# Attention backward and weight gradients: from two blocks under a scheduler to one hand-set order of slots

## The chip, the cores and the metric

One core of a Trainium2 chip runs the whole program. The metric is device time in microseconds (us) of one execution. Five engines take part, each with a queue of its own: TensorE (PE in the profile, its weight loads PEld), VectorE (DVE), ScalarE (ACT), GpSimd (POOL) and SyncE (SP), which issues most of the transfers.

## The reference

The forward pass of one block (layer norm, attention, residual, layer norm, MLP, residual) and the gradients of all its inputs. S = 2048 rows, D = 512, 32 heads of 16, F = 1792. Attention looks at 8 earlier positions, every second one:

```
idx  = pos[:, None] - off[None, :]          # off = 0, 2, ..., 14
kg, vg = k[:, :, idx], v[:, :, idx]
logits = einsum("bhsd,bhswd->bhsw", q, kg) * scale      # masked where idx < 0
o      = einsum("bhsw,bhswd->bhsd", softmax(logits), vg)
h      = x + o @ wo ;  h2 = h + gelu(ln(h) @ w1 + b1) @ w2 + b2
_out, _vjp = jax.vjp(_f, A_x, A_wqkv, A_wo, B_w1, B_b1, B_w2, B_b2)
```

The outputs are h2 and the gradients of x, wqkv, wo, w1, b1, w2 and b2.

## The kernel before

The rows are worked on in NC = 4 chunks of CH = 512. The program has a forward attention part, an MLP part (forward and backward, ending in `gh`, the gradient at h), and then the part that is changed: `p3_...`, the attention backward, and behind it the weight gradients. A scheduler sets the order of instructions on each engine from the order in which the code is written and from when buffers come free; engines wait on semaphores that it places.

Attention backward, for a chunk c:

- `p3_go(c)`: TensorE transposes `gh`, multiplies it with `woT` into `got` (features on partitions), and a row-major copy goes to `go_d` in HBM.
- `p3_gl(c, got)`: VectorE multiplies `got` with eight shifted views of `vw` (`dots`, tile `pr`, four of 4096 elements), TensorE sums over a head's features into `ps_ga`; `pp`, a row sum on TensorE, and `glf`, the gradient of the logits.
- `band`: the sums over the eight positions. A band is 256 rows; there are 2 each for the gradients of q, v and k of a chunk, 24 in all. SP loads `R`, 1.3 MB of shifted rows, in 4 transfers, into one of 3 buffers. VectorE multiplies `R` with coefficients `cf` (four of 2048 elements, tile `prb`, in two halves m), TensorE sums them with `S32`, ScalarE evicts into `gqs` or `gks`, which POOL's queue stores to `g3_d`. `coefs` makes `cf` by transposing pieces of `attn`, `glf` or `sh` on VectorE; `sh` is a copy shifted by position, four transfers (`p3_shift`).
- `p3_gq(c)`: the q bands. `p3_kv(c, shs)`: the v and k bands, `unperm` (transposes on TensorE) into `gqkvT`, then for each 128 rows 12 matmuls with `wqkvT` into `ps_gl1`, and `ln_bwd`: ScalarE makes `gyr`, POOL a small constant, VectorE four passes that end in `gx`, which SP stores.

The weight gradients each are sums over all 16 row tiles. gw2 (14 groups of 16 matmuls, lhs a tile `gtm` of 1 MB that a transposing transfer makes from `g_d`), gb2, gw1 (28 groups of 16 matmuls with 256 columns, tiles `ghm`), gwo (4 groups) and gwq (12 groups, from `g3_d`). `load_tm` loads the other operand, 2 MB, into the one buffer `r16`: `gout_r`, `ln2_r`, `o_r` and, in 32 transfers, `ln1_r`. `wg_out` evicts a group into one of two `gwst` buffers, and SP stores it. Transposed tiles have two buffers.

In the order as built, all of the weight gradients stand behind the last `ps_gl1` on TensorE. SP's queue holds, in one order, the loads of `R`, the shifts, the stores of `go_d`, `gx` and `gwst`, and the transposing loads; each of them waits there for what it needs.

## Time and profile before

| | |
|---|---|
| median of 3 runs | 985.37 us (985.09 to 988.18) |
| the profiled execution | 986.06 us, its span 984.1 us |
| mean granted TensorE clock | 0.835 |
| busy in the span | PE 695.0, DVE 535.2, ACT 336.1, POOL 87.3 us |
| moved by DMA | 146.09 MB, 148 GB/s on average |

The span runs from the first to the last instruction; durations of the trace belong to that one execution. The granted clock is a share of TensorE's full speed, and the DMA share is the mean busy share of the core's 16 DMA engines. A row of instructions has its start, its duration, engine, line, operation, result and operands, a count where several are merged, and in brackets the idle time before it and what ended that.

### The profile page before, as it was taken

To read this page: it belongs to the slowest core of one execution; us is meant where nothing else is said; L and a number is where in the kernel's file an instruction comes from. 1 tells how busy PE (TensorE), PEld (TensorE's weight loads), DVE (VectorE), ACT (ScalarE), POOL (GpSimd) and SP (SyncE) were. 2 spreads that over 40 slices of the span, in tenths; PEclk is the share of its full clock that TensorE was granted. 3 is DMA by queue.
4 is the path that set the end of the run, shared out by engine and by line. 5 is a ranking of instruction groups with operands and counts; after the bars stand their busy time and mean duration, and the time that the engine had idled before them with its cause. 6 is when DMAs were issued, how large, how long until landed. Compare 5 with 4: busy or idle time off the path is not lost.

```text
span 984.1 us, 10416 instructions
## 1 busy us (share of the span) xinstructions
PE 695.0 (71%) x3891; PEld 312.4 (32%) x3948; DVE 535.2 (54%) x814; ACT 336.1 (34%) x497; POOL 87.3 (9%) x137
## 2 busy tenths in 40 slices
PE   5777775547899898898556546537459775776788
PEld 2423332212334333333222212212114333664233
DVE  6778676458777787857767767777683000000000
ACT  2755664365346353414333233213222101111011
POOL 3211221200010010101000100100101000000000
PEclk9998897677999999999675785755659997997779
DMA  9646556851233242238848747747799986563211
GB/s 311 202 127 161 132 167 176 183 129 60 81 97 97 77 126 87 86 124 189 195 100 203 186 110 196 181 105 186 182 263 243 251 203 177 124 144 105 74 60 38
DMA packets 159599, 146.09 MB, mean 148 GB/s; under 512 B 96042, under 2 KB 150140, under 8 KB 155068
## 3 DMA queue, kind: packets, MB, share of 16 engines
q1 hardware_dynamic: 153196, 124.42, 49.2%
q0 software_dynamic: 6352, 20.99, 6.7%
q8 instruction: 31, 0.51, 0.2%
q14 instruction: 20, 0.16, 0.1%
HBM read 72.95 MB, written 47.80 MB: 123 GB/s over the span
## 4 chain that ended last, share of the span: by engine, by line
PE 29%; DMA 16%; DVE 10%; issue 5%; ACT 4%; SPq 4%; POOL 1%; DVEq 0%; ACTq 0%; POOLq 0%
DMA R<-q_d 5%; PE ps_gw L722 5%; PE ps_gw L707 4%; PE ps_gwq L755 4%; PE ps_gl L671 4%; DMA R<-go_d 3%; PE ps_f L533 2%; DVE prb L267 2%; DMA gtm<-g_d 2%; SPq L746 2%; PE ps_gg L546 2%; PE ps_gwo L729 2%; DMA R<-k_d 2%; DVE pr L236 2%; PE ps_go L612 1%
## 5 line engine op out<-in xcount | busy, mean ns | idle before, releaser
L267 DVE TENSOR_TENSOR prb<-R,cf 128x2048 bf16<-128x2048 bf16 x128 | 148.3, 1218 | 51.5 <-DMA R<-go_d 23.3
L272 PE MATMUL ps_band<-prb,S 128*32 128x512 bf16 x512 | 73.6, 564 | 116.3 <-DVE prb L267 113.2
L498 PE MATMUL ps_h<-ln2T,w 128*128 128x512 bf16 x223 | 63.4, 410 | 25.9 <-ACT x L501 22.4
L722 PE MATMUL ps_gw<-ghm,ln_r 128*128 128x256 bf16 x448 | 53.5, 284 | 22.3 <-ACT gwst L692 12.2
L272 PEld LDWEIGHTS <-S 128*32 128x32 bf16 x512 | 15.9, 100 | 162.1 <-DVE prb L267 105.5
L546 PE MATMUL ps_gg<-goT,w2T 128*128 128x512 bf16 x218 | 53.8, 378 | 11.4 <-DVE gb1p L549 8.6
L707 PE MATMUL ps_gw<-gout_r,gtm 128*128 128x512 bf16 x220 | 51.9, 396 | 12.9 <-DMA gtm<-g_d 12.7
L692 ACT ACTIVATE gwst<-ps_gw 128x256 bf16<-128x256 f32 (+1 forms) x42 | 18.5, 454 | 121.5 <-PE ps_gw L722 40.3
L755 PE MATMUL ps_gwq<-gtm,ln_r 128*128 128x512 bf16 x188 | 50.3, 427 | 9.9 <-DMA ln_r<-ln_d 9.7
L722 PEld LDWEIGHTS <-ln_r 128*128 128x128 bf16 x448 | 45.5, 102 | 30.5 <-issue 13.1
L533 PE MATMUL ps_f<-w,gt 128*128 128x512 bf16 x217 | 53.5, 383 | 1.1 <-DVE gt L510 0.5
L500 ACT ACTIVATE xb<-ps_h,b1c 128x512 bf16<-128x512 f32 x56 | 38.2, 685 | 45.5 <-PE ps_h L498 44.1
L330 PE MATMUL ps_qkv<-ln1T,wqkv 128*128 128x512 bf16 x184 | 47.5, 393 | 6.9 <-ACT kt L332 3.2
L671 PE MATMUL ps_gl<-wqkvT,gqkvT 128*128 128x512 bf16 x184 | 48.0, 414 | 0.2
L661 ACT ACTIVATE gks<-ps_band 128x512 bf16<-128x512 f32 x32 | 19.2, 600 | 82.7 <-PE ps_band L272 80.3
L208 ACT ACTIVATE gyr<-ps_gl,rstd 128x512 bf16<-128x512 f32 x32 | 21.9, 686 | 59.8 <-PE ps_gl L559 24.0
L498 PEld LDWEIGHTS <-w 128*128 128x128 bf16 x224 | 23.0, 103 | 60.0 <-issue 42.2
L501 ACT ACTIVATE x<-ps_h,b1c 128x512 bf16<-128x512 f32 x56 | 37.9, 684 | 9.0 <-DMA ln_d<-ln 6.9
L214 POOL TENSOR_SCALAR c<-sg 128x1 f32<-128x1 f32 x32 | 24.6, 769 | 172.7 <-ACT gyr L208 172.7
L236 DVE TENSOR_TENSOR pr<-qt,kt 128x4096 bf16<-128x4096 bf16 x16 | 36.0, 2284 | 5.7 <-ACT qt L332 3.5
L236 DVE TENSOR_TENSOR pr<-got,vw 128x4096 bf16<-128x4096 bf16 x16 | 35.6, 2287 | 1.3 <-DMA vw<-vf_d 1.3
L707 PEld LDWEIGHTS <-gtm 128*128 128x128 bf16 x224 | 22.4, 101 | 41.9 <-DMA gtm<-g_d 13.8
(312 smaller groups left out, 1080.2 us busy)
## 6 DMA issues: line engine op xcount, KB each, us to landing
R<-v_d SPq DMA_DIRECT2D x32, 320.0 KB, 5.0
R<-k_d SPq DMA_DIRECT2D x32, 320.0 KB, 5.1
R<-go_d SPq DMA_DIRECT2D x32, 320.0 KB, 7.5
R<-q_d SPq DMA_DIRECT2D x32, 320.0 KB, 10.8
g_d<-gt SPq DMA_DIRECT2D x12, 512.0 KB, 3.2
ln_d<-ln POOLq DMA_DIRECT2D x8, 512.0 KB, 6.0
out_dram<-gwst SPq DMA_DIRECT2D x30, 128.0 KB, 1.7
w<-in_B_w_dram POOLq DMA_DIRECT2D x2, 1792.0 KB, 11.2
```

Source lines behind the costliest of these rows:

```text
L236: V.tensor_tensor(out=pr[:], in0=ql[:, g, :].unsqueeze(1).to_broadcast([P, W, 512]), in1=_sub(kw_[:, g, PAD:PAD + 512], [[-DIL, W], [1, 51 ...
L267: V.tensor_tensor(out=pr[:, hf].rearrange("p j (d h) -> p j d h", h=H), in0=R[:, o:o + 4, :].rearrange("p j (d h) -> p j d h", h=H), in1=c ...
L272: T.matmul(ps[32 * j:32 * j + 32, :], lhsT=S32[:], rhs=pr[:, hf, j, :], start=(hf == 0), stop=(hf == 1), skip_group_check=True)
L330: T.matmul(ps[:, gg, :], lhsT=wqkv[:, dc, sel * D + g * P:sel * D + (g + 1) * P], rhs=st_[c]["ln1T"][:, dc, :], start=(dc == 0), stop=(dc ...
L498: T.matmul(ps[:, i, :], lhsT=w1[:, dc, f * P:(f + 1) * P], rhs=ln2T[c][:, dc, :], start=(dc == 0), stop=(dc == DC - 1))
L500: A.activation(out=xb[:, f - f0, :], in_=ps[:, i, :], func=ACT.Identity, bias=b1c[:, f:f + 1])
L533: T.matmul(ps[:], lhsT=gts[f // 4][:, f % 4, j * P:(j + 1) * P], rhs=w2[:, f, :], start=(f == 0), stop=False)
L546: T.matmul(ps[:, i, :], lhsT=w2T[:, dc, f * P:(f + 1) * P], rhs=goT[:, dc, :], start=(dc == 0), stop=(dc == DC - 1))
L671: T.matmul(ps[:], lhsT=gqkvT[:, b, j * P:(j + 1) * P], rhs=wqkvT[:, b, :], start=(b == 0), stop=(b == 11))
L707: T.matmul(ps[:], lhsT=gtm[:, t, (f % 2) * P:(f % 2 + 1) * P], rhs=r16[:, t, :], start=(t == 0), stop=(t == NT - 1))
L722: T.matmul(ps[:, 0:256], lhsT=r16[:, t, dc * P:(dc + 1) * P], rhs=ghm[:, t, :], start=(t == 0), stop=(t == NT - 1))
L755: T.matmul(ps[:], lhsT=r16[:, t, dc * P:(dc + 1) * P], rhs=g_[:, t, :], start=(t == 0), stop=(t == NT - 1))
```

## The change

The forward coefficients and those of the backward pass are transposed by fewer, larger instructions: `coefs` makes all of a chunk at once, in one instruction of 1024 elements from `sh`, in two of 512 from `glf` or `attn`.

Everything from the attention backward on stands in a manual schedule, so the order on each engine is that of the code. The code is written in slots. A slot has some VectorE work (one `dots` tile or one half band), then `slot(dve_us)`: it first runs the TensorE work that `later` put off to this slot (a band's sums, `unperm`, `p3_go` in pieces, `ps_gl1`), each with a cost, and then `filler`, which takes matmuls from the generator `wgrads` until `dve_us * 1.22` less those costs is used up. `wgrads` runs through gw2, gb2, gw1, gwo and gwq; a number that it yields is charged, 24.0, 14.0 or 6.0 after it has issued loads, and a name ("q", "v", "k") holds it until that gradient is stored. At the end `filler(1000.0)` issues the rest.

`ln_bwd` of chunk c-2 is spread over the dots of chunk c (`gln1`); chunks 2 and 3 have none over them. v bands come first, then q, then k; `R` is loaded two bands ahead (`load_R`). The stores of `gx`, of `gwst` and of gb1 are issued by POOL. gwq takes its second operand in halves of 1 MB in the buffers of the transposed tiles, where before all three were loaded into buffers of their own while gw2 ran.

```diff
+    def coefs(wp, src, off, hs):
+        cf = wp.tile([P, 2, 2, 8, H], BF16, name="cf", tag="cf", bufs=2)
+        if hs == 512:
+            V.transpose(out=cf[:].rearrange("p a b c h -> p (a b c h)"), in_=_sub(src, [[256, 4], [1, 8], [8, 32]], off))
+        else:
+            for hf in range(2):
+                V.transpose(out=cf[:, hf].rearrange("p b c h -> p (b c h)"),
+                            in_=_sub(src, [[256, 2], [1, 8], [8, 32]], off + hf * hs))
         return cf
...
+    ms = tc.manual_schedule()
+    ms.__enter__()
...
+    def wg_out(ps, dst, width=D, sca=1.0):
+        st = gwp.tile([P, D], BF16, name="gwst", tag="gwst", bufs=2)
+        A.activation(out=st[:, 0:width], in_=ps[:, 0:width], func=ACT.Copy, scale=sca)
+        G.dma_start(out=dst, in_=st[:, 0:width])
...
+    def load_t(src):
+        t_ = gwp.tile([P, NT, 256], BF16, name="gwm", tag="gwm", bufs=2)
+        SY.dma_start_transpose(out=t_[:], in_=src)
+        return t_
...
+    MM = 0.22
+
+    def wgrads():
+        r16 = load_tm("gout_r", gof)
+        tiles = [load_t(g_d[f * 256:(f + 1) * 256, :]) for f in range(2)]
+        yield 24.0
+        for f in range(FT):
+            gtm = tiles[f // 2]
+            ps = FY("ps_gw2")
+            for t in range(NT):
+                T.matmul(ps[:], lhsT=gtm[:, t, (f % 2) * P:(f % 2 + 1) * P], rhs=r16[:, t, :], start=(t == 0), stop=(t == NT - 1))
+                yield MM
+            if f % 2 == 1:
+                n = f // 2 + 2
+                tiles.append(load_t(g_d[n * 256:(n + 1) * 256, :] if n < 7 else gh_d[(n - 7) * 256:(n - 6) * 256, :]))
+            wg_out(ps, out_6[f * P:(f + 1) * P, :], D, 0.5)
+        ps = FY("ps_gb2")
+        for t in range(NT):
+            T.matmul(ps[0:1, :], lhsT=ones_col[:], rhs=r16[:, t, :], start=(t == 0), stop=(t == NT - 1))
...
+        tiles = tiles[7:]
+        for q in range(7):
+            ghm = tiles[q]
+            for dc in range(DC):
+                ps = FY("ps_gw1")
+                for t in range(NT):
+                    T.matmul(ps[:, 0:256], lhsT=r16[:, t, dc * P:(dc + 1) * P], rhs=ghm[:, t, :],
+                             start=(t == 0), stop=(t == NT - 1))
+                    yield MM / 2
+                if dc == DC - 1:
+                    if q + 2 < 7:
+                        tiles.append(load_t(gh_d[(q + 2) * 256:(q + 3) * 256, :]))
+                    if q == 6:
+                        r16 = load_tm("o_r", o_d)
+                wg_out(ps, out_4[dc * P:(dc + 1) * P, q * 256:(q + 1) * 256], 256)
...
+        r16 = gwp.tile([P, NT, D], BF16, name="ln1_r", tag="r16", bufs=1)
+        for sc in range(NC * 2):
+            for j, ap in enumerate(perm_rows(ln1_d, sc * 256, sc)):
+                SY.dma_start(out=r16[32 * j:32 * j + 32, 2 * sc:2 * sc + 2, :], in_=ap)
+        HN = NT // 2
+
+        def half(sel, i):
+            t_ = gwp.tile([P, HN, D], BF16, name="gqh", tag="gwm", bufs=2)
+            SY.dma_start(out=t_[:], in_=g3_d[sel][:, i * HN:(i + 1) * HN, :])
+            return t_
+        yield "q"
+        hv = [half(0, 0), half(0, 1)]
+        yield 14.0
+        for si, sel in enumerate((0, 2, 1)):
+            for d2 in range(2):
+                pss = [FY("ps_gwq") for _ in range(2)]
+                for i in range(2):
+                    for dd in range(2):
+                        dc = 2 * d2 + dd
+                        for t in range(HN):
+                            T.matmul(pss[dd][:], lhsT=r16[:, i * HN + t, dc * P:(dc + 1) * P], rhs=hv[i][:, t, :],
+                                     start=(i == 0 and t == 0), stop=(i == 1 and t == HN - 1))
+                            yield MM
+                        if i == 1:
+                            wg_out(pss[dd], out_2[dc * P:(dc + 1) * P, sel * D:(sel + 1) * D])
+            if si < 2:
+                yield ("v", "k")[si]
+                hv = [half((2, 1)[si], 0), half((2, 1)[si], 1)]
+                yield 6.0
+
+    fill = wgrads()
...
+    RATIO = 1.22
+    pend = []
+
+    def later(n, cost, fn):
+        pend.append([n, cost, fn])
+
+    def slot(dve_us):
+        pe = 0.0
+        for x in list(pend):
+            x[0] -= 1
+            if x[0] <= 0:
+                pend.remove(x)
+                x[2]()
+                pe += x[1]
+        filler(dve_us * RATIO - pe)
...
+    def load_R():
+        if rpos[0] >= len(bands):
+            return
+        kind, c, sc = bands[rpos[0]]
...
+        R = p3.tile([P, 10, 512], BF16, name="R", tag="rows", bufs=3)
+        for w4 in range(4):
+            r = row0 + (-4 * w4 - 2 if kind == "q" else 4 * w4)
+            SY.dma_start(out=R[32 * w4:32 * w4 + 32].rearrange("p a d -> p (a d)"),
+                         in_=_ap(d_t[r:r + 1, :], [[8 * D, 32], [1, 10 * D]]))
+        rq.append(R)
+
+    def band_tile(kind, c, sc, m, cf, gs, sca, after):
+        if m == 0:
+            load_R()
+            bt["R"] = rq.pop(0)
+        R = bt["R"]
...
+        def pe():
...
+            A.activation(out=gs[:, m, :].rearrange("p (h d) -> p h d", d=DH), in_=natural(ps), func=ACT.Copy, scale=sca)
+            if m == 1:
+                sel = dict(q=0, k=1, v=2)[kind]
+                G.dma_start(out=g3_d[sel][:, 4 * c + 2 * sc:4 * c + 2 * sc + 2, :], in_=gs[:])
+                if after:
+                    later(1, 1.0, after)
+        later(1, 0.7, pe)
+        slot(2.45)
...
+    def gln1(c, j):
+        d = st3[c]
+        t = c * TPC + j
+
+        def pe():
             ps = Y("ps_gl1")
             for b in range(12):
-                T.matmul(ps[:], lhsT=gqkvT[:, b, j * P:(j + 1) * P], rhs=wqkvT[:, b, :], start=(b == 0), stop=(b == 11))
-            t = c * TPC + j
+                T.matmul(ps[:], lhsT=gqkv[c][:, b, j * P:(j + 1) * P], rhs=wqkvT[:, b, :], start=(b == 0), stop=(b == 11))
+            d["gyr"] = ln_bwd_a(p3, ps[:], rstd1[:, t:t + 1])
+
+        def dve():
             gx = p3.tile([P, D], BF16, name="gx", tag="gx", bufs=2)
-            ln_bwd(p3, ps[:], ln1[:, j, :], rstd1[:, t:t + 1], gh_all[c][:, j, :], gx[:])
-            SY.dma_start(out=gxf[t * P:(t + 1) * P, :], in_=gx[:])
-
-    got = p3_go(0)
-    for c in range(NC):
-        p3_gl(c, got)
+            ln_bwd_v(p3, *d["gyr"], d["ln1"][:, j, :], gh_all[c][:, j, :], gx[:])
+            G.dma_start(out=gxf[t * P:(t + 1) * P, :], in_=gx[:])
+            if j == TPC - 1 and c + 1 < NC:
+                load_ln1(c + 1)
+        later(2, 0.0, dve)
+        later(1, 2.65, pe)
...
+    for c in range(NC + 2):
+        if c >= 2:
+            gln1(c - 2, 0)
...
+                if c >= 2 and g > 0:
+                    gln1(c - 2, g)
+                slot(2.3 + (1.9 if c >= 2 else 0))
+            if c + 1 < NC:
+                load_vw(c + 1)
+            if c == 0:
+                p3_go(1)
+        elif c >= 2:
+            slot(2.0)
+            for g in range(1, 4):
+                gln1(c - 2, g)
+                slot(2.0)
+            slot(2.0)
+            slot(2.0)
+            slot(2.0)
+        if c == NC + 1:
...
+        if c < NC:
+            V.tensor_tensor(out=glf[:, :, c * CH:(c + 1) * CH], in0=L[:], in1=ac, op=ALU.mult)
+            cfq = coefs(p3, glf[:, 0, 0:1], c * CH, SP)
+        if c > 0:
+            shk = shift(c - 1, glf)
+            vtile(2)
+            vtile(3)
+        if c == NC:
+            later(1, 0.0, lambda: open_gates.add("v"))
+        if 0 < c < NC - 1:
+            p3_go(c + 1)
+        if c < NC:
+            st3[c]["sh"] = shift(c, attn)
+            gqs[c] = []
+            for k in range(4):
+                sc, m = k // 2, k % 2
+                if m == 0:
+                    gqs[c].append(p3.tile([P, 2, 512], BF16, name="gqs", tag="gqs", bufs=2))
+                band_tile("q", c, sc, m, cfq, gqs[c][sc], scale, None)
+            if c == NC - 1:
+                later(2, 0.0, lambda: open_gates.add("q"))
+        if c > 0:
+            cfk = coefs(p3, shk[:, 0, 0:1], 0, 512)
+            for k in range(4):
+                sc, m = k // 2, k % 2
+                if m == 0:
+                    bt["gs"] = p3.tile([P, 2, 512], BF16, name="gks", tag="gks", bufs=2)
+                gs = bt["gs"]
+                band_tile("k", c - 1, sc, m, cfk, gs, scale,
+                          lambda gs=gs, sc=sc, c=c: unperm(gs[:], gqkv[c - 1][:, 4:8, :], 4, sc * 256))
+            if c == NC:
+                slot(0.5)
+                slot(0.5)
+                open_gates.add("k")
...
+    G.dma_start(out=out_5.rearrange("(f p) -> f p", p=P), in_=gb1s[:])
+    filler(1000.0)
...
-        SY.dma_start(out=dst, in_=st[:, 0:width])
-        g_ = end.tile([P, NT, D], BF16, name=f"gtm{sel}")
-        SY.dma_start(out=g_[:], in_=g3_d[sel][:])
```

Counted in the order as built, gw2 and gb2 (240 matmuls) and 116 of gw1's 448 now stand before the last `ps_gl1` on TensorE; 332 of gw1, gwo (64) and gwq (192) stand behind it.

SP's queue in the attention part, about chunk 2. `R` are a band's rows, `sh` the shifted copies, `gx` the gradient of x. Before:

```order
L647 DMA sh<-attn 32x2x512 x4
L260 DMA R<-go_d 32x5120 x4
L647 DMA sh<-glf 32x2x512 x4
L260 DMA R<-go_d 32x5120 x4
L260 DMA R<-q_d 32x5120 x8
L175 DMA ln1r<-ln_d 128x4x512
L260 DMA R<-k_d 32x5120 x3
L675 DMA out_dram<-gx 128x512
```

And now:

```order
L627 DMA_TRANSPOSE gwm<-g_d 128x16x256
L830 DMA sh<-attn 32x2x512 x4
L768 DMA R<-q_d 32x5120 x8
L238 DMA go_d<-tmst 128x2x512 x2
L768 DMA R<-go_d 32x5120 x4
L627 DMA_TRANSPOSE gwm<-g_d 128x16x256
L768 DMA R<-go_d 32x5120 x4
```

The stores of `gx` are gone from between the loads of `R`, the shift of `glf` stands between other loads, and transposing loads for the weight gradients have come in.

VectorE at the layer norm of chunk 1 (`junk`, `sx`, `u`, `gx`), which ends the work on that chunk. Before:

```order
L267 TENSOR_TENSOR prb<-R,cf 128x2048 x4
L250 STREAM_TRANSPOSE cf<-glf 128x256 x2
L211 ISA junk,sx<-gyr,ln1r 128x512
L211 ISA sx 128x1
L216 TENSOR_SCALAR u<-ln1r,sx,c_4804 128x512
L217 TENSOR_TENSOR u<-u,gh_2800 128x512
L218 TENSOR_TENSOR gx<-u,gyr 128x512
```

And now, with the dots of chunk 3 (`pr`):

```order
L780 TENSOR_TENSOR prb<-R,cf 128x2048 x8
L877 TENSOR_TENSOR pr<-got,vw 128x4096 x2
L216 ISA junk,sx<-gyr,ln1r 128x512
L216 ISA sx 128x1
L219 TENSOR_SCALAR u<-ln1r,sx,c_5058 128x512
L220 TENSOR_TENSOR u<-u,gh_2788 128x512
L221 TENSOR_TENSOR gx<-u,gyr 128x512
L877 TENSOR_TENSOR pr<-got,vw 128x4096
```

The layer norm has moved from behind the bands of its own chunk to between the dots two chunks on.

SP's queue at the end of the program, from the last tiles of gw1 on. Before:

```order
L697 DMA o_r<-o_d 128x16x512
L693 DMA out_dram<-gwst 128x256
L693 DMA out_dram<-gwst 128x512 x3
L746 DMA ln_r<-ln_d 32x2x512
L693 DMA out_dram<-gwst 128x512
L746 DMA ln_r<-ln_d 32x2x512 x31
L693 DMA out_dram<-gwst 128x512 x12
```

And now:

```order
L627 DMA_TRANSPOSE gwm<-gh_d 128x16x256 x5
L622 DMA o_r<-o_d 128x16x512
L681 DMA ln_r<-ln_d 32x2x512 x32
L686 DMA gqh<-gq_d 128x4096 x2
L686 DMA gqh<-gv_d 128x4096 x2
L686 DMA gqh<-gk_d 128x4096 x2
```

The stores have left the queue, and the six halves of gwq's operands stand behind the 32 loads of `ln1_r`.

More of the change, by code (lines that the diff above doesn't have):

```diff
@@ new lines, with filler @@
+    fill = wgrads()
+    fs = dict(debt=0.0, gate=None, done=False)
+    open_gates = set()
+    def filler(us):
+        fs["debt"] += us
+        while fs["debt"] > 0 and not fs["done"]:
+            if fs["gate"] is not None:
+                if fs["gate"] not in open_gates:
+                    fs["debt"] = 0.0
+                    return
+                fs["gate"] = None
+            x = next(fill, None)
+            if x is None:
+                fs["done"] = True
+            elif isinstance(x, str):
+                fs["gate"] = x
+            else:
+                fs["debt"] -= x
@@ L645, in p3_shift, with t, shift @@
+        def t():
+            to_tm_store(p3, got, 0, go_d, c * CH, 2)
+        later(1, 1.0, a)
+        later(2, 1.8, b(0))
+        later(3, 1.8, b(2))
+        later(4, 1.0, t)
+    def shift(c, src):
         sh = p3.tile([P, 2, 512], BF16, name="sh", tag="sh", bufs=2)
@@ L649, in p3_shift, with load_ln1 @@
         return sh
[L651 to L668 removed]
+    def load_ln1(c):
+        st3[c]["ln1"] = p3.tile([P, TPC, D], BF16, name="ln1r", tag="ln1r", bufs=1)
+        load_rows(st3[c]["ln1"], ln1_d, c)
@@ L700 @@
-    r16 = load_tm("gout_r", gof)
-    for f in range(FT):
-        if f % 2 == 0:
-            gtm = gwp.tile([P, NT, 256], BF16, name="gtm", tag="gwm", bufs=2)
-            SY.dma_start_transpose(out=gtm[:], in_=g_d[f * P:(f + 2) * P, :])
-        ps = FY("ps_gw2")
-        for t in range(NT):
-            T.matmul(ps[:], lhsT=gtm[:, t, (f % 2) * P:(f % 2 + 1) * P], rhs=r16[:, t, :], start=(t == 0), stop=(t == NT - 1))
-        wg_out(ps, out_6[f * P:(f + 1) * P, :], D, 0.5)
-    ps = FY("ps_gb2")
```

241 lines of the change are left out of this document (128 added, 113 removed).

## The prediction

> **What bounds the kernel now.** I read the page's slices first, then the same span cut into stretches, then the chain that ended last, then the waits of VectorE and of SP's queue.
>
> ```profile
> PE 695.0 (71%) x3891; PEld 312.4 (32%) x3948; DVE 535.2 (54%) x814; ACT 336.1 (34%) x497; POOL 87.3 (9%) x137
> PE   5777775547899898898556546537459775776788
> ...
> DVE  6778676458777787857767767777683000000000
> ...
> PEclk9998897677999999999675785755659997997779
> DMA  9646556851233242238848747747799986563211
> ```
>
> TensorE is busy 71% of the span, but in the last quarter VectorE has nothing to do, and in the quarter before it TensorE is half idle at a granted clock of 0.5 to 0.8. The cut at the two seams (first matmul of `p3_go`, first weight-gradient matmul) gives numbers; columns are length, busy time of PE, PEld, DVE, ACT, POOL, then granted clock, DMA share and GB/s.
>
> ```profile
> 457.40:751.00 293.60, 169.77 (x1073) 67.25 (x1087) 211.01 (x244) 86.30 (x132) 23.79 (x39) 0.66 0.72 177
> 751.00:984.10 233.10, 175.86 (x935) 95.42 (x943) 2.37 (x7) 29.58 (x62) 0.25 (x1) 0.88 0.52 135
> 829.50:895.20 65.70, 53.46 (x448) 45.54 (x448) 0.00 (x0) 9.80 (x27) 0.00 (x0) 0.94 0.48 108
> 895.20:920.40 25.20, 16.61 (x62) 6.89 (x64) 0.00 (x0) 2.17 (x4) 0.00 (x0) 0.80 0.32 101
> 920.40:943.20 22.80, 13.15 (x29) 3.07 (x30) 0.00 (x0) 0.60 (x1) 0.00 (x0) 0.56 0.33 98
> ```
>
> I call 457.4 to 751.0 the stage (attention backward) and 751.0 to 984.1 the tail (weight gradients: gw2 and gb2, then gw1 from 829.5, gwo from 895.2, gwq from 920.4). They follow each other, though they use different engines. In the stage VectorE works 211 of 293.6 us. The waits there (engine, waiter, releaser; total, times, longest):
>
> ```profile
> DVE junk L211 <- ACT gyr L208: 25.8, 15, 6.2
> DVE prb L267 <- DMA R<-go_d: 23.3, 5, 7.2
> DVE prb L267 <- DMA R<-k_d: 8.6, 2, 4.5
> DVE prb L267 <- issue: 8.4, 4, 4.0
> ...
> SPq L675 <- DVE gx L218: 72.3, 12, 18.1
> SPq L647 <- DVE glf L629: 54.4, 3, 19.1
> ```
>
> Some 40 us go to row tiles `R` that are not there and 26 to the layer-norm backward. The last two rows say why `R` is late: SP's queue stands behind a `gx` store or a shift of `glf`, and the `R` loads stand behind those.
>
> **The change part by part.**
>
> Start. Order up to 457.4 hardly moves (some merged transposes in the forward part): 0.
>
> The stage, floor by VectorE. Its work stays: 211.0 in the stage and 2.4 just behind. The 48 coefficient transposes become 8 of four times and 8 of twice the size.
>
> ```profile
> L250 DVE STREAM_TRANSPOSE cf<-sh x32: 584/600/639, 497.1 to 726.1; 128x256 bf16<-128x256 bf16 x32
> L267 DVE TENSOR_TENSOR prb<-R,cf 128x2048 bf16<-128x2048 bf16 x96 | 111.3, 1220 | 43.8 <-DMA R<-go_d 23.3 <-DMA R<-k_d 8.6 <-issue 8.4
> L236 DVE TENSOR_TENSOR pr<-got,vw 128x4096 bf16<-128x4096 bf16 x16 | 35.6, 2287 | 1.3 <-DMA vw<-vf_d 1.3
> 743.31 0.69 ACT L208 ACTIVATE gyr<-ps_gl,rstd 128x512 bf16<-128x512 f32 x1 [0.64 <-PE ps_gl L671]
> ...
> 744.12 0.69 DVE L211 CUSTOM_DVE_ANT_0 junk<-gyr,ln1r 128x512 bf16<-128x512 bf16 x1 [6.22 <-ACT gyr L208]
> ...
> 745.83 0.43 DVE L218 TENSOR_TENSOR gx<-u,gyr 128x512 bf16<-128x512 bf16 x1
> 745.90 0.69 ACT L208 ACTIVATE gyr<-ps_gl,rstd 128x512 bf16<-128x512 f32 x1 [1.81 <-issue]
> ```
>
> No row has the larger transposes. Were time all per element, 48 x 0.600 = 28.8 stay; were it all per instruction, 16 x 0.6 = 9.6. The nearest doubling is 1220 to 2287 ns, a factor of 1.87; so 8 x 0.6 x 1.87 x 1.87 + 8 x 0.6 x 1.87 = 25.8, a gain of 3 (ends 0 and 19). Floor: 213.4 - 3 = 210. To it come waits that the new order keeps: the layer norm of chunks 2 and 3 has no dots beside it any more. Each such run costs the 6.2 in the row of `junk` and then three times some 0.5 us, since a `gyr` comes every 2.6 us (743.31 to 745.90) and VectorE takes 2.1 for one (744.12 to 746.26); 8 each, 16. With 4 at the start (the first `got`, the row sums of chunk 0, which have no band tile over them) the floor is 230 us.
>
> The stage, by the transfers. DMA is 0.72 busy over 293.6 us: 211 us of all 16 engines. The same loads stay, and more come in: ten transposed 1 MB tiles are issued inside the stage, where before two were at its end; `ln2_r` (2 MB); 14 gradient stores of 128 KB.
>
> ```profile
> L704 SPq DMA_TRANSPOSE gtm<-g_d x7: 4640/5121/18177, 725.5 to 798.9; - x7
> DMA to landing us min/median/max: 6.9/7.1/8.2
> o_r<-o_d SPq DMA_DIRECT2D x1, 2048.0 KB, 8.2
> gtm<-gk_d SPq DMA_DIRECT2D x1, 2048.0 KB, 9.8
> 517.29 12.35 DMA R<-q_d
> ```
>
> A plain 2 MB lands in 8.2, so 4.1 per MB; a transposed tile lands in 7.1. What it takes from the others lies between; I take 5.5. So 8 more tiles are 44, `ln2_r` 8, the stores 1.8 MB x 4.1 = 7: 211 + 59 = 270 us. The two tile loads of `R<-q_d` (2.6 MB) need 12.35 us together, 6.2 each, where VectorE uses a band up in 4 x 1.16 plus its coefficients, 5.2: with transposes between, the transfers set the pace of the bands. I take 260, nearer to 270 than to 230, since only three `R` buffers let transfers run ahead in the dots. The stage ends at 717.4 instead of 751.0.
>
> The Trainium skill (Advanced Engine Details and Errata, X-Bar Transpose) states that transposing DMAs are as fast as regular ones. By it the tile is 4.1, the transfers sum to 259, and 250 for the stage would give 858; the trace has 7.1 against 4.1, so it does not agree.
>
> The tail. gw2, gb2 and the load of `ln2_r` (751.0 to 829.5) leave it, with 116 of gw1's 448 matmuls; 332 stay behind the last ps_gl1.
>
> ```profile
> 845.92 7.15 PE L722 MATMUL ps_gw<-ghm,ln_r 128*128 128x256 bf16 x64 [1.70 <-ACT gwst L692]
> 856.53 7.15 PE L722 MATMUL ps_gw<-ghm,ln_r 128*128 128x256 bf16 x64 [3.46 <-ACT gwst L692]
> 920.39 0.60 SPq L746 DMA_DIRECT2D ln_r<-ln_d  x1
> 921.66 19.65 SPq L746 DMA_DIRECT2D ln_r<-ln_d  x31
> 943.17 37.42 PE L755 MATMUL ps_gwq<-gtm,ln_r 128*128 128x512 bf16 x160 [0.61 <-DMA ln_r<-ln_d]
> ...
> 980.67 0.60 ACT L692 ACTIVATE gwst<-ps_gwq 128x512 bf16<-128x512 f32 x1 [2.86 <-PE ps_gwq L755]
> ```
>
> TensorE does not bind the stage: to its 169.8 us, at clock 0.66, come 240 matmuls of gw2 and gb2 at 37.42/160 = 0.234 and 116 of gw1 at 7.15/64 = 0.112, 69; were these at 0.66 too, 105, it would be 274 with every wait filled, and at a higher clock less.
>
> gw1: at the old pace 65.7 x 332/448 = 48.7; without the waits 332/64 x 7.15 = 37.1. The waits came from stores that stood behind a transpose on SP; they move to POOL's queue, but a tile's load (7.1) is as long as a tile's matmuls, so I take 43. `o_r` and gwo: 25.2 as before. gwq loses something: its operands were loaded early, and now the two 1 MB halves stand on SP behind the 32 `ln1_r` loads. Those end 20.9 us after gwo; a half lands in 9.8/2 = 4.9; the first matmul comes at 25.8, where before 32 were done at 22.8. Then 192 x 37.42/160 = 44.9. At two changes of operand the second half can load only when its buffer's last matmul is done, 16 matmuls (3.7) hide part of 4.9, between 1 and 5 us each, 3 taken: 6. End: 3.5, as from 980.67 on, the store now by POOL. Sum: 43 + 25.2 + 25.8 + 44.9 + 6 + 3.5 = 148.4 instead of 233.1.
>
> Together 717.4 + 148.4 = 865.8 of span. The profiled execution took 986.06 with a span of 984.1, 0.7 above the median of 985.37; with that 2 us, 867.
>
> **The rivals.**
>
> - VectorE sets the stage: `R` is in time. For it: without a `gx` store ahead of them on SP the loads start when a buffer frees, two bands early (10 us). Against: 12.35 us for two. 230 + 148: 838.
> - Stores by POOL are slow.
>
> ```profile
> gv_d<-gks POOLq DMA_DIRECT2D x8, 256.0 KB, 9.4
> out_dram<-h2s POOLq DMA_DIRECT2D x16, 128.0 KB, 2.0
> out_dram<-gx SPq DMA_DIRECT2D x16, 128.0 KB, 1.7
> L664 POOL DMA_DIRECT2D gv_d<-gks x8: 540/540/543, 510.6 to 727.1; - x8
> ```
>
> At 9.4 for `gx` with two buffers, the third and fourth of a run wait: 9.9 - 2 x 2.6 = 4.7 each in the two uncovered runs, about 1 in the others; 23 in all: 890. Against: 128 KB, half of `gv_d`.
> The Trainium skill (SBUF — State Buffer, SBUF: two separate sides) has a rule that speaks for it: VectorE in a two-port mode keeps GpSimd from writing descriptors, some 2.5 us for a store by its example; as an estimate 16 x 2.5 = 40 us, or 907. The issue took 540 ns beside VectorE, every time, so the trace shows none of it.
> - The transposes hold SP. The first one held the queue 18.2 us while other loads were under way (maximum above), later ones 5. Behind it `R` loads wait. At 11, about midway between the two, eight of them on top of 230 give 318 and 925; two bands of lead (10.4 us) less the 6.2 of a tile leave some 4 to take it up.
> - Slower than before: the same mechanism at its full price. 8 x 18.2 = 146 on 230 puts the stage's end at 833, with the tail 981 of span, 983; from about 18.5 us a tile it is slower. Against: the 18.2 had 2 MB of `gout_r` and two `R` tiles queued ahead, which comes once, at the start.
> - The clock of 0.66 stays, and TensorE sets the stage: 274 against 260, 881; inside the forecast. Against: the tail, where TensorE is dense, has 0.88. That the matmuls don't move is excluded by the order.
>
> **How the numbers follow.** Forecast (stage 245 to 278, so 850 to 885) 0.60; VectorE's pace 0.15; POOL's stores 0.08; SP held 0.12; slower 0.03; within 0.3%, which is about what a measurement here can tell from no change, 0.02. Time 867. The range 832 to 912 holds the first three and the nearer end of SP held; the rest is under 0.2. Faster 0.95, same 0.02, slower 0.03.
>
> **What would show it.** In the profile after, the last ps_gl1 matmul at about 717; VectorE idle before `prb` on R some 30 us; DMA share in the stage above 0.9; about 148 us from there to the end, with gwq's first matmul some 26 us behind gwo's last. Wrong: `R` waits under 10 us (then 838), SP rows of transposes over 10 us with `prb` waiting behind (then above 900), `gx` waiting on its own store.

## The result, and the profile after

The changed kernel takes 904.78 us (901.73 to 909.35) beside 985.77 for the kernel before on the same chip: a ratio of 0.9178, interval 0.9136 to 0.922. The forecast was 867 with a range of 832 to 912. The direction and the range held; of a gain of 118 us, 81 came, and the time lies above the 850 to 885 that the forecast gave as its own. The profiled execution took 901.73 with a span of 899.9, so the comparison of places is against the forecast's span of 865.8.

The page of the changed kernel, busy time and slices:

```profile
PE 659.8 (73%) x3890; PEld 303.7 (34%) x3948; DVE 531.7 (59%) x774; ACT 335.2 (37%) x497; POOL 126.3 (14%) x213
...
PE   4785874655688989988975479779777597862585
...
DVE  6786685545876868669476877957965751000000
...
PEclk9996988767899999999996579988986799987798
DMA  8645566584213223324399999999999845532351
```

The transfers now stand at 9 for eleven slices on end (the stage), where before three did, and VectorE's empty tail has shrunk from nine slices to six. The same span is cut at the seams (stage; then gw1, `o_r` and gwo, the wait for gwq, gwq, the end). Columns are length, busy time of PE, PEld, DVE, ACT, POOL, then granted clock, DMA share and GB/s:

```profile
460.60:744.60 284.00, 212.15 (x1427) 93.99 (x1446) 208.38 (x214) 97.20 (x155) 41.02 (x75) 0.83 0.97 229
744.60:791.70 47.10, 38.81 (x333) 33.05 (x331) 2.73 (x9) 8.46 (x23) 12.28 (x24) 0.96 0.52 122
791.70:815.90 24.20, 15.29 (x62) 6.54 (x64) 0.00 (x0) 2.17 (x4) 2.62 (x5) 0.86 0.33 108
815.90:841.90 26.00, 0.02 (x1) 0.05 (x2) 0.00 (x0) 0.60 (x1) 0.54 (x1) 0.59 0.46 145
841.90:889.80 47.90, 43.30 (x188) 18.81 (x192) 0.00 (x0) 6.57 (x11) 5.94 (x11) 0.97 0.37 127
889.80:899.90 10.10, 0.01 (x1) 0.00 (x0) 0.00 (x0) 0.60 (x1) 0.54 (x1) 0.62 0.07 26
```

Against before, the stage got only 9.6 us shorter (293.6 to 284.0) but took 356 matmuls of the weight gradients in (TensorE 169.8 to 212.2 busy, its granted clock 0.66 to 0.83), and the tail went from 233.1 to 155.3. VectorE's work in the stage is 208.4, so it waits 75 us there. The list says on what (engine, waiter, releaser; total, times, longest), from just ahead of the stage to just behind it:

```profile
DVE junk L216 <- ACT gyr L208: 29.0, 15, 7.9
DVE prb L780 <- DMA R<-q_d: 22.2, 7, 8.6
DVE pr L877 <- DMA vw<-vf_d: 8.1, 2, 7.0
DVE prb L780 <- DMA R<-k_d: 5.7, 3, 3.6
DVE glf L938 <- PE ps_ga L930: 4.2, 1, 4.2
DVE gx L221 <- DMA out_dram<-gx: 4.1, 1, 4.1
```

Loads that are late (R 27.9, `vw` 8.1) and the layer-norm backward (`gyr` 29.0) carry it, as forecast in kind. In the tail:

```profile
ACT gwst L617 <- DMA out_dram<-gwst: 27.9, 11, 7.1
PE ps_gwq L698 <- DMA gqh<-gq_d: 26.0, 1, 26.0
...
PE ps_gwo L674 <- DMA o_r<-o_d: 8.7, 1, 8.7
PE ps_gw L661 <- ACT gwst L617: 8.2, 4, 4.2
```

By its parts the forecast missed 34.1 us of span: the start 3.2 later, the stage 24.0 longer, the tail 6.9 longer. (The forecast's seam at 457.4 is not quite the first matmul of `p3_go`: two stand at 456.5, as the first two now stand at 460.6. Like for like the start came 4.1 later and the stage got 10.5 shorter.) The experiments ask for each of the three.

### The profile page after: what moved, and what is told of

The parts are those of the page before. It is cut to its first block, busy times and chain, and to the rows that moved or that the text cites. A ratio compares the mean times of both kernels' runs of the same rounds, so it can differ in the third digit from the quotient of the medians.

```text
span 899.9 us, 10402 instructions
## 1 busy us (share of the span) xinstructions
PE 659.8 (73%) x3890; PEld 303.7 (34%) x3948; DVE 531.7 (59%) x774; ACT 335.2 (37%) x497; POOL 126.3 (14%) x213
## 5 line engine op out<-in xcount | busy, mean ns | idle before, releaser
L780 DVE TENSOR_TENSOR prb<-R,cf 128x2048 bf16<-128x2048 bf16 x96 | 110.8, 1219 | 28.4 <-DMA R<-q_d 22.2
L788 PE MATMUL ps_band<-prb,S 128*32 128x512 bf16 x384 | 42.7, 473 | 48.2 <-DVE prb L780 47.2
L698 PE MATMUL ps_gwq<-gqh,ln_r 128*128 128x512 bf16 x188 | 43.3, 387 | 30.6 <-DMA gqh<-gq_d 26.0
L661 PE MATMUL ps_gw<-gwm,ln_r 128*128 128x256 bf16 x448 | 54.1, 280 | 8.9 <-ACT gwst L617 8.9
L640 PE MATMUL ps_gw<-gout_r,gwm 128*128 128x512 bf16 x212 | 57.3, 411 | 1.8 <-issue 1.7
L618 POOL DMA_DIRECT2D out_dram<-gwst x58 | 31.4, 542 | 150.1 <-ACT gwst L617 143.2
L845 PE MATMUL ps_gl<-wqkvT,gqkvT 128*128 128x512 bf16 x188 | 44.5, 390 | 0.3 <-issue 0.2
L210 POOL TENSOR_SCALAR c<-sg 128x1 f32<-128x1 f32 x32 | 21.9, 686 | 159.8 <-ACT gyr L208 159.6
```

The costliest lines, as they stand in the source:

```text
L618: G.dma_start(out=dst, in_=st[:, 0:width])
L640: T.matmul(ps[:], lhsT=gtm[:, t, (f % 2) * P:(f % 2 + 1) * P], rhs=r16[:, t, :], start=(t == 0), stop=(t == NT - 1))
L661: T.matmul(ps[:, 0:256], lhsT=r16[:, t, dc * P:(dc + 1) * P], rhs=ghm[:, t, :], start=(t == 0), stop=(t == NT - 1))
L698: T.matmul(pss[dd][:], lhsT=r16[:, i * HN + t, dc * P:(dc + 1) * P], rhs=hv[i][:, t, :], start=(i == 0 and t == 0), stop=(i == 1 and t == ...
L780: V.tensor_tensor(out=pr[:, hf].rearrange("p j (d h) -> p j d h", h=H), in0=R[:, o:o + 4, :].rearrange("p j (d h) -> p j d h", h=H), in1=c ...
L788: T.matmul(ps[32 * j:32 * j + 32, :], lhsT=S32[:], rhs=pr[:, hf, j, :], start=(hf == 0), stop=(hf == 1), skip_group_check=True)
```

## The experiments

Four theories stood for the stage: the transfers at their bytes set it (A); the place of 1 MB loads on SP, ahead of what VectorE needs next (B); fill matmuls ahead of `ps_gl1` and `ps_band` on TensorE (C); or the new order itself is longer than the 230 us that the forecast put as VectorE's floor (D). Times and ratios are each against the kernel before on the same chip. The stage is read from one profile a kernel; the changed kernel profiled a second time, as the control, gave 287.8 where the first gave 284.0, so differences under 4 us between stages say nothing.

### The control

> The changed kernel again, unaltered, beside the kernel before and the next two on one chip, so that edits worth a few microseconds are read against it and not against a run on another chip. Every theory expects 902 to 907 and a ratio of 0.914 to 0.920 to the kernel before.

906.97 us, ratio 0.917 (0.9145 to 0.9195), which repeats the first result.

### The order alone, without the fill

```diff
-        filler(dve_us * RATIO - pe)
+        pass
```

> The hand order alone: no gradient matmul, no load of its operands and no gradient store comes before the last band; everything of the weight gradients runs behind it. In the changed kernel the stage (first got to last ps_gl1) was 284 us at a DMA share of 0.96 and PE 0.75 busy. If the transfers set it (some 60 of the 274 us of transfer time in it were the fill's), or the loads behind transposes on SP, or the fill matmuls that delay gyr: all three expect about 235 to 245 here, near the floor of 230 that VectorE sets, and a tail longer by the 69 us of moved matmuls and some 10 of loads, so about 930. If the stage is held by the new order itself (uncovered layer norms, two bands of lead not enough), it stays above 265 and the time is above 955.

957.97 us, ratio 0.9709 (0.9678 to 0.9741). The stage and the tail of this kernel, and what VectorE waits for:

```profile
460.90:712.90 252.00, 168.21 (x1088) 68.08 (x1087) 207.81 (x214) 87.46 (x133) 30.90 (x53) 0.71 0.84 208
712.90:953.70 240.80, 166.68 (x946) 93.70 (x945) 3.07 (x9) 30.17 (x62) 33.76 (x63) 0.88 0.51 130
```

```profile
DVE junk L216 <- ACT gyr L208: 24.4, 12, 7.5
DVE prb L780 <- DMA R<-q_d: 6.4, 5, 1.6
DVE glf L938 <- PE ps_ga L930: 5.1, 1, 5.1
DVE prb L780 <- PE ps_band L788: 3.6, 3, 1.8
```

No gradient matmul is in this stage. Of the gradients' loads `gout_r` and two tiles are: they stand next on SP and are issued from 685.9 on, behind the last load of R, as they were at the end of the stage before. The stage is 252, between the two outcomes that were expected, and not the 230 of the forecast: theory D has 22 us of the 24 that the stage missed. VectorE's 208 is what the forecast had (210); its own waits are 44 where the forecast allowed 20. The order alone is worth 29 us (and its tail is 7.7 longer than before); the fill is worth the other 52 or so.

### Taking load from the stage: three ways

Operand tiles loaded twice and used again for all others:

```diff
     def load_t(src):
+        if len(lt) >= 2:
+            lt.append(lt[-2])
+            return lt[-1]
```

> The same matmuls in the same places, but the transposed operand tiles are loaded only twice and used again for all others (gw2 and gw1 are then computed from the first two tiles only): 12 transposing loads of 1 MB are gone, about 8 of them from the stage. Transfers: 8 x 5.5 = 44 us less in a stage that has no slack there, 284 becomes 240 to 250. SP held by transposes: also about 240 to 250, and no row of a transpose above 10 us but the first two. TensorE (fill matmuls ahead of ps_gl1 and of ps_band): the stage stays at 275 to 284, since every matmul is still there. The tail loses a few us of gw1's waits (47 to about 40).

The row tile loaded for every second band only:

```diff
+        if sc == 1:
+            rq.append(None)
+            return
         R = p3.tile([P, 10, 512], BF16, name="R", tag="rows", bufs=3)
...
-            bt["R"] = rq.pop(0)
+            bt["R"] = rq.pop(0) or bt["R"]
```

> The row tile R is loaded only for the first half of each chunk's band and used again for the second half (so the second half of q, k and v gradients is computed from the wrong rows): 12 of 24 bands load nothing, some 72 us of transfer time less, while every transposing load and every matmul stays. Transfers set the stage: 284 becomes about 245 (VectorE's 230 and what the fill costs it). SP held by transposes: 255 to 265, since the waits behind a transpose stay but only every second band can meet one. TensorE: 275 to 284, unchanged.

Plain loads in place of transposing ones:

```diff
-        SY.dma_start_transpose(out=t_[:], in_=src)
+        SY.dma_start(out=t_[:], in_=src.rearrange("(p a) (b d) -> p (a b) d", a=2, d=256))
```

> The 14 transposed operand tiles are loaded by plain loads of the same 1 MB (rows in the wrong layout, so gw2 and gw1 are computed from other values); bytes, matmuls and order stay. Transfers at their bytes alone: a plain MB costs 4.1 where I put the transposed one at 5.5, so 8 to 10 of them give back 11 to 14, stage 284 to about 270. SP held by transposes: the queue goes on at once, waits of prb on R fall from 28 to under 10 and the stage to 250 to 255. TensorE: unchanged at 280 to 284.

They took 880.5 us (ratio 0.8913, 0.8877 to 0.8948), 886.39 (0.899, 0.8954 to 0.9026) and 890.32 (0.9021, 0.8993 to 0.9048). Their stages, a row of each in this order:

```profile
460.70:726.90 266.20, 210.83 (x1446) 93.61 (x1446) 208.37 (x214) 97.17 (x155) 40.97 (x75) 0.86 0.83 214
```

```profile
461.30:725.60 264.30, 209.19 (x1447) 92.98 (x1447) 207.97 (x214) 97.50 (x155) 41.08 (x75) 0.86 0.75 187
```

```profile
462.60:737.50 274.90, 214.36 (x1446) 93.37 (x1446) 208.48 (x214) 97.22 (x155) 41.02 (x75) 0.84 0.88 237
```

The next table takes length times DMA share as the time of the transfers, and VectorE's waits from the same list as above. That time is a measure and not a floor: in the changed kernel the share reads 1.14 from 620 to 640 us, more than all of the engines' time.

| kernel | stage | transfers | waits on R | on `vw` | on `gyr` |
|---|---|---|---|---|---|
| changed | 284.0 | 275 | 27.9 | 8.1 | 29.0 |
| plain tile loads | 274.9 | 242 | 21.3 | 4.1 | 30.5 |
| two tile loads for ten | 266.2 | 221 | 13.0 | 4.7 | 28.4 |
| half the rows | 264.3 | 198 | 16.9 | 2.6 | 30.8 |
| no fill | 252.0 | 212 | 6.8 | 1.7 | 24.4 |

TensorE does the same in the first four (209 to 214 busy), so theory C can't explain the 9 to 20 us that they differ by. The stage follows the transfers' time down, but not one for one, and only to about 265: 33 us less gives 9, 54 less gives 18, 77 less gives 20. With plain loads 270 was expected for theory A and 250 to 255 for B, and 275 came; the other two were expected at 240 to 250 for A. The 12 to 14 us above the kernel without fill that are left there are not divided further (`gyr` waits 4 to 6 longer, R 6 to 10). The tails differ too: 9 us shorter with two tile loads, 4.6 with plain ones, 2 longer with half the rows.

What is left of the waits on R with half the rows is two, of 8.1 and 8.8 us. Both come where a tile load stands on SP ahead of the shift of `attn` and the load of R; the first:

```profile
577.73 5.03 SPq L627 DMA_TRANSPOSE gwm<-g_d  x1
...
585.38 2.18 SPq L771 DMA_DIRECT2D R<-q_d  x4
...
594.21 9.17 DVE L783 TENSOR_TENSOR prb<-R,cf 128x2048 bf16<-128x2048 bf16 x8 [8.14 <-DMA R<-q_d]
```

The two longest waits on R of the changed kernel (8.6 and 7.4) come at the same place, plain loads leave 6.5 and 6.2 there, and with two tile loads in all no wait on `R<-q_d` is above 2.0. So 77 us less of transfers left these two waits as they were, and theory B keeps some 16 us; 255 to 265 had been expected for it with half the rows, and 264 came. The DMA share is 0.94 from 577 to 594 us, where the first lies, so SP's queue and a local rush of loads can't be told apart there.

By this measure a transposing tile can be priced too. Eight taken out are 54 us of transfers, 6.8 each; made plain, all ten give 33 back, 3.4 each. The forecast had 5.5, between a landing of 7.1 and 4.1, half the landing of a plain 2 MB. A plain 1 MB landed here in 5.0 us at the least, a transposing one in 6.7. The Trainium skill (Advanced Engine Details and Errata, X-Bar Transpose), by which both should cost the same, is not borne out. How much dearer the transposing load is stays open: twice by the transfers' time, a third by the shortest landing.

### Moving the loads instead

Three buffers for the operand tiles, and the same loads at other places:

```diff
-        t_ = gwp.tile([P, NT, 256], BF16, name="gwm", tag="gwm", bufs=2)
+        t_ = gwp.tile([P, NT, 256], BF16, name="gwm", tag="gwm", bufs=3)
```

> The operand tiles gwm get three buffers instead of two: same bytes, same transposing loads, same matmuls in the same places, but a load goes to a buffer that has been free for a whole pair of row blocks, so SP does not stand at it until TensorE has used the tile before. In the changed kernel SP stood idle 104 us in the stage ahead of such loads (waits of up to 14.6 us), with the shift loads and R loads behind it. If that standing makes R late: prb's waits on R fall from 28 to under 15, vw's stay, the stage falls from 284 to 266 to 272, and gw1 in the tail loses its waits for tiles. If the number of bytes sets the stage (DMA share 0.96): R waits stay above 22 and the stage at 280 to 284. In the tail the changes of operand in gwq (2.3 and 2.1) vanish in either case.

904.56 us, ratio 0.9146 (0.9122 to 0.917): no gain that the intervals show. In the profile the stage is 293.7 at a DMA share of 1.02, and the tail 149.4. The tile loads by duration on SP, of the changed kernel, then of this one:

```profile
L627 SPq DMA_TRANSPOSE gwm<-g_d x7: 4374/6009/15132, 472.4 to 630.8; - x7
...
DMA to landing us min/median/max: 6.7/8.3/17.5
```

```profile
L627 SPq DMA_TRANSPOSE gwm<-g_d x7: 4658/11968/14664, 473.6 to 629.4; - x7
...
DMA to landing us min/median/max: 6.7/12.8/17.9
```

A load that no longer stands waiting for its buffer is issued while R loads are under way, and the seven then hold SP 12.0 us in the median instead of 6.0. Standing was exchanged for holding. The waits on R fell a little (27.9 to 22.0), and the last layer-norm run paid: its first `junk` waited 15.7, since matmuls of the fill stood ahead of `ps_gl1` on TensorE, two of them for a `gwst` buffer:

```profile
731.02 2.83 PE L661 MATMUL ps_gw<-gwm,ln_r 128*128 128x256 bf16 x16 [2.18 <-ACT gwst L617]
735.98 0.37 PE L661 MATMUL ps_gw<-gwm,ln_r 128*128 128x256 bf16 x1 [2.13 <-ACT gwst L617]
...
744.86 10.52 PE L845 MATMUL ps_gl<-wqkvT,gqkvT 128*128 128x512 bf16 x47
```

Placing them: the filler starts only behind the load of `vw` of chunk 1 (`fs`), and tile loads are held back (`hold`) from the shift of `glf` to the third q band tile, where `flush` issues them:

```diff
                 load_vw(c + 1)
+                fs["on"] = True
...
+            hold[0] = c < NC
...
                 band_tile("q", c, sc, m, cfq, gqs[c][sc], scale, None)
+                if k == 2:
+                    hold[0] = False
+                    flush()
```

> The same loads at other places on SP: the fill starts only behind the load of vw of chunk 1 (which stood behind 2 MB of gout_r and two transposed tiles), and a tile load that falls between the shift of glf and the third q band tile of a chunk is held back until that tile, so that it no longer stands ahead of the shift of attn and the two R<-q_d loads. If the place of 1 MB loads ahead of what VectorE needs next makes the waits: vw's 7.0 goes, the R<-q_d waits of 8.6 and 7.4 fall to about 2 each, and the stage is 284 - 19 = 265 or a few us above it. If the bytes set the stage wherever they stand: the waits come back at other bands, the stage stays at 280 to 285 and the time at 900 or more.

913.18 us, ratio 0.9241 (0.9214 to 0.9268), slower than the control by 6. The waits that were aimed at went, and came back elsewhere:

```profile
DVE junk L216 <- ACT gyr L208: 36.0, 15, 11.5
DVE prb L800 <- DMA R<-q_d: 8.0, 5, 2.4
DVE prb L800 <- PE pt L186: 7.0, 2, 4.5
DVE prb L800 <- DMA R<-go_d: 7.0, 3, 4.2
DVE prb L800 <- DMA R<-k_d: 6.4, 2, 3.9
DVE cf L257 <- DMA sh<-glf: 5.4, 1, 5.4
```

`vw` is no longer in the list and `R<-q_d` fell from 22.2 to 8.0, but `gyr`, `R<-go_d`, the shift and TensorE's queue took it over; the stage is 289.6, no different from the control's 287.8. With this many bytes in the stage, moving the loads moved the waits. That does not clear the queue: tile loads that neither stand nor hold SP, with all of their bytes kept (plain loads with a third buffer, say), were not run.

### The start

```diff
-        if sc == 0:
-            d["cf"] = coefs(late, attn[:, 0, 0:1], c * CH, SP)
+        d["cf"] = coefs_two(late, attn[:, 0, 0:1], c * CH, SP, sc)
```

`coefs_two` makes two transposes of 128x256 for each band, as in the kernel before.

> Only the forward part's coefficient transposes are put back to two of 128x256 for each half chunk, as before; attention backward keeps the merged ones. If the merged transposes in the forward part are why the first matmul of p3_go came at 460.6 to 462.6 us in the changed kernel and in four variants of it, where it was 457.4 before, it comes at 457 to 458 here and the time falls by about 3.5. If the later start has another cause (the scheduler of the forward part sees a different rest of the program, or runs differ), the start stays at 460 to 462 and the time is the same.

The first matmul of `p3_go`, before and in this kernel:

```profile
456.50 0.59 PE L612 MATMUL ps_go<-ghT,woT 128*128 128x512 bf16 x2 [1.91 <-ACT ghT L187]
```

```profile
455.50 0.59 PE L821 MATMUL ps_go<-ghT,woT 128*128 128x512 bf16 x2 [1.91 <-ACT ghT L187]
```

It comes at 455.5 instead of 460.6; with the same edit in the last kernel below it comes at 456.2, and in all the others between 459.7 and 462.7. So the merged transposes in the forward part are why it was late, though they are fewer. That 2 x 1.06 us now stand ahead of a chunk's first band, where 2 x 0.61 stood ahead of each, may be the reason; it was not tested. The stage ends at 742.9, where two profiles of the changed kernel have 744.6 and 748.9, so how much of the 5 us reaches its end can't be read. 902.02 us, ratio 0.9125 (0.9098 to 0.9152); the interval overlaps the control's.

### The tail

```diff
-        st = gwp.tile([P, D], BF16, name="gwst", tag="gwst", bufs=2)
+        st = gwp.tile([P, D], BF16, name="gwst", tag="gwst", bufs=4)
...
-            gx = p3.tile([P, D], BF16, name="gx", tag="gx", bufs=2)
+            gx = p3.tile([P, D], BF16, name="gx", tag="gx", bufs=4)
```

> gwst and gx get four buffers instead of two; stores stay on POOL. If the slower landing of POOL's stores (4.2 and 6.2 us against 1.7 by SP before) costs time through the two buffers: the wait of gx on its own store (4.1 us) goes, ACT's waits on the store of gwst in the tail (27.9 us, of which TensorE sees 8.2 to 8.9) go, gw1 in the tail takes 39 to 41 instead of 47, and the time falls by 8 to 12. If TensorE or the load of the next tile sets gw1 anyway, gw1 stays at 45 or more and the time falls by under 4.

896.26 us, ratio 0.9074 (0.9047 to 0.9101). gw1 behind the stage:

```profile
742.70:783.30 40.60, 36.85 (x334) 32.09 (x331) 2.76 (x9) 8.67 (x23) 12.77 (x24) 1.00 0.65 142
```

40.6 instead of 47.1, and no wait of `gx` on its store is left in the stage (281.6): stores that land later than before, through only two buffers, were the wait. The 64 KB stores of gw1 landed in 3.8 us in the median and `gx` in 6.2, both 1.7 by SP before. That POOL issues them is not the whole reason: without the fill its stores of `gx` in the stage landed in 2.1.

```diff
-            wg_out(ps, out_3[k * P:(k + 1) * P, :])
+            wg_out(ps, out_3[k * P:(k + 1) * P, :], eng=SY)
...
-                            wg_out(pss[dd], out_2[dc * P:(dc + 1) * P, sel * D:(sel + 1) * D])
+                            wg_out(pss[dd], out_2[dc * P:(dc + 1) * P, sel * D:(sel + 1) * D], eng=SY)
```

> The stores of gwo and gwq (the last 16) go out by SP instead of POOL; all others stay on POOL. The changed kernel and its variants end 10.0 us after the last eviction starts, the kernel before 3.4. If the last store by POOL is what makes it 10, the end comes 3.5 to 4.5 after the last eviction and the time falls by 6. If it is the end of the program that takes longer with more POOL work, the end stays at 10 and the time too.

913.64 us, ratio 0.9246 (0.9222 to 0.9271): slower. The span ends at 911.0, 3.5 behind the start of the last eviction, where it was 10.0 in the changed kernel, so the longer end goes with a last store by POOL:

```profile
907.48 0.60 ACT L617 ACTIVATE gwst<-ps_gwq 128x512 bf16<-128x512 f32 x1 [1.13 <-PE ps_gwq L698]
```

But the stores stood ahead of the next halves on SP, and a change of operand took 6.5, where it took 2.3 and 2.1 in the changed kernel, a mechanism that was not expected for this run. TensorE's matmuls of gwq took 5.4 us more as well (48.7 to 43.3), at granted clocks of 0.82 to 0.90 instead of 0.91 to 1.00:

```profile
868.52 16.91 PE L698 MATMUL ps_gwq<-gqh,ln_r 128*128 128x512 bf16 x63 [6.61 <-DMA gqh<-gv_d]
891.93 15.45 PE L698 MATMUL ps_gwq<-gqh,ln_r 128*128 128x512 bf16 x62 [6.51 <-DMA gqh<-gk_d]
```

Then `ln1_r` in fewer loads behind the halves, and only the last four stores by SP:

```diff
-        for sc in range(NC * 2):
-            for j, ap in enumerate(perm_rows(ln1_d, sc * 256, sc)):
-                SY.dma_start(out=r16[32 * j:32 * j + 32, 2 * sc:2 * sc + 2, :], in_=ap)
+        for m in range(2):
+            for j in range(4):
+                SY.dma_start(out=r16[32 * j:32 * j + 32, m::2, :],
+                             in_=_ap(ln1_d[j + 4 * m:j + 4 * m + 1, :], [[8 * D, 32], [256 * D, NC * 2], [1, D]]))
...
-                            wg_out(pss[dd], out_2[dc * P:(dc + 1) * P, sel * D:(sel + 1) * D])
+                            wg_out(pss[dd], out_2[dc * P:(dc + 1) * P, sel * D:(sel + 1) * D], eng=SY if si == 2 else G)
```

> Only the tail: ln1_r is loaded in 8 loads of 256 KB instead of 32 of 64 KB, behind the two halves of gwq's first operand instead of ahead of them, and the last four stores go by SP. If SP's issue of 32 loads, 0.63 each, and then the halves are what gwq waits 26.0 for: 8 x 0.63 and a landing of 2 MB as of o_r (8.6) leave 9 to 10, a gain of 16. If the 2 MB in 1 KB rows need the time themselves, the wait stays at 20 or more. The end comes 3.6 instead of 10.0 after the last eviction (the run with gwo's and gwq's stores on SP had 3.6, and lost it by stores ahead of the next halves). In all 903 - 22 = 881.

887.11 us, ratio 0.896 (0.8934 to 0.8986), 20 us less than the control.

```profile
828.67 0.58 PE L699 MATMUL ps_gwq<-gqh,ln_r 128*128 128x512 bf16 x1 [8.52 <-DMA ln_r<-ln_d]
833.50 16.71 PE L699 MATMUL ps_gwq<-gqh,ln_r 128*128 128x512 bf16 x63 [4.26 <-DMA ln_r<-ln_d]
```

gwq waits 12.8 instead of 26.0, in two pieces, where 9 to 10 were expected, and the end is 3.3 behind the start of the last eviction.

### What gained, together

The edits of the store buffers, the start and the tail in one kernel.

> The edits that gained, together: the tail as in the run with ln1_r in 8 loads (907.0 to 887.1 there, 20), four buffers for gwst and gx (ratio to the kernel before 0.907 against 0.917 of the changed kernel unaltered, 10), the forward part's old coefficient transposes (0.9125 against 0.917, 4). If they lie one behind the other on the path, as the places say (tail's gwq and end; tail's gw1; start): 907 - 34 = 873 and a ratio of 0.882. If the transfers of the stage take back what the start and the gx buffers gain, as they did in part: 876 to 882.

875.22 us (872.82 to 876.75), ratio 0.8854 (0.883 to 0.8877), better than both kernels.

```profile
456.20:743.40 287.20, 216.45 (x1427) 95.25 (x1446) 208.57 (x214) 97.61 (x155) 41.34 (x75) 0.82 0.97 227
743.40:874.10 130.70, 98.08 (x583) 58.46 (x587) 2.72 (x9) 18.59 (x40) 19.77 (x37) 0.91 0.51 142
```

The tail went from 155.3 to 130.7 and kept its gain. The stage of 287 is no different from the control's (287.8); it starts at 456.2 instead of 461.1 and ends at 743.4 instead of 748.9.

## Why the prediction was right, and where it was off

- **The mechanism.** Weight-gradient matmuls run beside VectorE's stage, at a higher clock, and the transfers fill up; VectorE waits on R some 30 us (27.9) and the DMA share is above 0.9 (0.97). All as said, but the last `ps_gl1` came at 744.6 and not at 717. Without the fill the gain would have been 29.
- **The transfers' sum.** 211 for the order's own and 270 with the fill; 212 and 275 measured. The tile at 5.5 was 6.8 by this measure, and the rest of the fill 9 instead of 15: that the sum stood is in part luck. What it stands for is weaker than the forecast took it to be: with three buffers and one tile more in the stage, the same measure gives 300 (293.7 x 1.02).
- **The step that failed: the floor by VectorE.** "210 + 16 for two uncovered runs + 4 at the start" is 252, not 230. VectorE's work (208) and the two uncovered runs (7.8 and some 9 in the kernel without fill) were right. Missing were the covered runs, where `gyr` comes late as well (some 6), waits on R (6.8), a band's sums (3.6) and half of the start, where `vw`, `pp` and `glf` waited 1.7, 1.1 and 5.1.
- **"I take 260, nearer to 270 than to 230".** That choice between floor and transfers failed too. With the measured 252 and 275 it would give some 269, and 284 came, above both. The fill brought 63 us of transfers and made the stage 32 us longer, about half of that: waits on R are 21 us longer than without the fill, on `vw` 6, on `gyr` 5, on `gx`'s store 4, and those on a band's sums 4 shorter. The forecast's 260 was 30 above its own floor, so the size of this step was near, but not for the reason given.
- **The start** was put at 0 and came 3.2 later (4.1 like for like), by the merged transposes in the forward part. Their own price was right: 16.1 and 8.2 us against 18.2 and 9.1 before, a gain of 3.0.

```profile
L257 DVE STREAM_TRANSPOSE cf<-sh 128x1024 bf16<-128x1024 bf16 x8 | 16.1, 2009 | 0.0
...
L260 DVE STREAM_TRANSPOSE cf<-glf 128x512 bf16<-128x512 bf16 x8 | 8.2, 1064 | 0.1
```

- **The tail.** gw1 47.1 (43), `o_r` and gwo 24.2 (25.2), gwq's wait 26.0 (25.8), gwq with its changes of operand 47.9 (50.9), the end 10.1 (3.5). The two that were off are both stores by POOL: in gw1 through two buffers, at the end by the last one. That one landed 2.0 us after its issue; what fills the rest of the 10 us is not shown.
- **The rivals.** POOL's stores were named, but for `gx`, where 4.1 came once; most of their price stood in the tail, 6.5 in gw1 and 6.5 at the end. The rule of the Trainium skill (SBUF — State Buffer, SBUF: two separate sides) that VectorE keeps GpSimd from writing descriptors is not seen to cost anything: without the fill the stores of `gx` in the stage landed in 2.1 us beside the same work on VectorE. No run tells whether that work is in a two-port mode. SP held by transposing loads is real (4.1 to 15.1 us a tile beside 0.34 in the median for a plain one), and the forecast's sign of it came in part: the time is above 900, and `prb` waits 16 us at two places behind these loads, though they hold SP for 5.4 and 5.6 us there and not over 10. But moving them in two ways gained nothing, and making them plain took 9 off the stage, where the rival had 58 more than the forecast's 260. VectorE's pace (838) and TensorE at a clock of 0.66 (881) did not come, nor did a loss.

## What to carry to other kernels

When work is put under a stage, work out that stage's floor with all its own waits (run the order without the fill if you can), and don't take the larger of floor and transfers as the answer: here about half of the transfer time that the fill brought came on top of the floor. Where a bulk load shares a queue with urgent loads, look at the waits one by one: here fewer bytes and cheaper transfers gained, other places for the loads did not, and two waits behind bulk loads stayed when half of the urgent loads were taken out. Stores that land later need more buffers, and the last store of a program is worth a look of its own.

## What the runs showed of the hardware that I had not expected

- The time that a transposing load of 1 MB holds its queue depends on what is under way: 6.0 us in the median of seven when most had first stood waiting for a buffer, 12.0 when most were issued close behind R loads; a plain load of the same 1 MB took 0.34 in the median.
- A last store by POOL ends the program 10.0 to 10.1 us after the last eviction starts, in ten profiles, though the store lands 2.0 us after its issue where that was read; by SP it is 3.3 to 3.5.
- TensorE's granted clock in the stage rose with its busy share: 0.66 at 58% before, 0.71 at 67% in the new order without fill, 0.83 at 75% with it.
- The DMA share reads above 1 where transfers crowd (1.14 from 620 to 640 us), so length times share is no fixed price of the bytes.
